# Recurrent attention with a gated layer behind it: transposes of eleven units as DMA transfers in SyncE's queue, and a new order of all stages

## The chip, the core and the metric

The kernel runs on one core of one Trainium2 chip. The metric is device microseconds of one execution (lower is better). Engines: TensorE (PE in the profile; PEld is its weight load), VectorE (DVE), ScalarE (ACT), GpSimd (POOL) and SyncE (SP), which here only issues DMA transfers. One program execution was profiled; its span is the time from the first to the last instruction.

## The reference

Two stages. The first is a linear recurrence for 4 batches, 8 heads, 768 steps and head width 48; the second is a feed-forward layer on the first one's output, 3072 tokens by 384, hidden width 1024.

```
for t in range(S):                     # r, k, v, w: [4, 8, 768, 48], u: [8, 48]
    y[t]  = r[t] @ (state + (u * k[t]) outer v[t])
    state = w[t] * state + k[t] outer v[t]
x  = y as [3072, 384]
h  = x @ w_in                          # [3072, 1024]
s  = h * softmax(h)
ln = (s - mean(s)) / sqrt(var(s) + 1e-6) * g_ln
out = ln @ w_out                       # [3072, 384]
```

## The kernel before

**Tiling.** Time is cut into 6 chunks of 128 steps, and a chunk of one batch is a unit: 24 units, unit i being chunk i // 4 of batch i % 4. All 8 heads of a unit are worked on at once. A unit's stages, by the names that the order uses:

- LW, LK, LR, LV (`load_w`, `load_k`, `load_r`, `load_v`): four transfers of 192 KB in pieces of 48 floats, from SP's queue, into rings of 7 buffers (NIO).
- lw (logarithm, ACT), cum (two products with triangular matrices on PE, the running sums), ex (exponential, ACT), kp (`scaled`, DVE: k and r times the decays, bf16, into a ring of 6 buffers, NKP).
- krk and krr (`transposed`): four PE products each with the identity, which turn the scaled k and r, two heads at a time, into PSUM; kr (`transposed_copy`): a copy of the 128 by 1024 result to SBUF into a ring of 6 buffers, on ACT (".a") or DVE (".d"). These three are the stage that the change touches.
- M (`scores`): eight PE products of turned k with turned r; m (`scores_copy`): to SBUF, on DVE with the causal mask, or on ACT, and then sel (`scores_mask`) on POOL applies the mask.
- p, q, dg, dv: the term with u (POOL, POOL, DVE, POOL); vb (`v_cast`): v to bf16.
- Y (`attend`): turned r times state, plus scores times v, in PSUM; y adds dv (".n") or, with ".i", PE adds it with an identity product. S, et, st: the state of the batch for its next chunk (not needed for the last four units).
- X and xT: y turned by PE and copied; H (24 PE products), e (exponential, ACT), he (DVE), hq (square, on ACT, DVE or POOL): the hidden layer; Oa and Ob (`output`): 36 PE products that give the layer's output, its mean and its sums; sq, qm, lv, o: the scaling; out: the store of 192 KB, SP's queue.

Ahead of the units there are the weights: LI (three transfers of `w_in`) and wi (casts), LO (two of `w_out`), gw (its rows times the gain), mn and mc (their column mean) and ce (the mean taken off, eight pieces). No Oa can start before its rows of `w_out` went through LO, gw, mn, mc and ce, and no H before LI and wi. "hot" is a number of idle PE products.

**What sets the order.** `ORDER` is one list of words, written out; the loop at the end of the kernel (line 512) calls one function per word. Each engine carries out its own instructions in the order of the list (`InOrder`, line 84 and 87: every line of the profile has one of these two numbers, so groups are told apart by tiles). SP's queue holds loads and stores in one order, and a store waits there for its `o`, with all that stands behind it. Each transfer in SP's queue also waits for the completion of the one eight places ahead of it.

Of the kernel before, what the change touches and what calls it, by code (L numbers as in the profile page):

```python
# [9 lines left out]
BF16 = mybir.dt.bfloat16  # L10
# [5 lines left out]
ALU = mybir.AluOpType  # L16
# [2 lines left out]


ORDER = """
LW0 LK0 hot3.s3 LR0 LU0 LG0 lw0 LW1 cum0.b0 LK1 hot1.s3 LV0 LR1 p0 us0.s0 LW2 gs0.s3 hot2.s2 LK2 uc0 gc0 ex0 q0
LI0 LR2 lw1 kp0 LW3 cum1.b1 hot1.s3 vb0.a dg0 LV1 ex1 S0.s1 LK3 krk0.s2 p1 hot3.s3 LR3 kp1 LI1 lw2 krk1.s0 LI2
krr0 cum2.b0 LV2 kr0.d hot1.s3 LO0 M0.b1 krr1 LO1 m0.d hot3.s3 kr1.a LW4 LK4 p2 et0 ex2 M1.b1 LR4 hot4.s3 LW5
dv0 kp2 lw3 LV3 Y0.is3 m1.d vb1.p LK5 krk2.s2 y0.a q1 LR5 krr2 wi0.a cum3.b0 LW6 S1.s0 q2 dg1 X0.s3 LV4 ex3 st0
dv1 LK6 dg2 kr2.a kp3 LR6 Y1.is1 LW7 y1.a krk3.s2 LV5 et1 wi1.a krr3 X1.s1 LK7 wi2.d M2.b1 LR7 xT1.a p3 xT0.d
m2.d LW8 H0.b0 LV6 vb2.p kr3.d LK8 dv2 H1.b1 e0 st1 LR8 gw3.p LW9 gw0.p he0 S2.s1 LK9 e1 Y2.is3 q3 LR9 hot3.s2
et2 gw2.p LV7 y2.a dg3 gw7.a gw1.p X2.s2 LW10 he1 M3.b0 gw4.p LV8 lw4 gw6.p LK10 m3.d hq0.a gw5.p cum4.b1 LR10
mn0.s0 ex4 LW11 hq1.d LV9 xT2.a p4 kp4 mc0 H2.b0 lw5 ce7.d ce0.d ce3.d ce5.d krk4.s3 vb3.a cum5.b1 ce4.d e2
ce6.d krr4 S3.s2 ce1.d ce2.d st2 dv3 ex5 Oa0.s0 kr4.a q4 kp5 Y3.is1 Ob0 p5 et3 he2 lw6 y3.a krk5.s3 cum6.b1 sq0  # L30
q5 X3.s1 st3 ex6 M4.b0 qm0 krr5 xT3.d vb4.p Oa1.s2 m4.d kr5.a S4.s1 p6 lv0 kp6 M5.b0 o0.a Ob1 dg4 lw7 out0 et4
dg5 krk6.s3 m5.a dv4 cum7.b1 LK11 st4 Y4.ns0 LR11 krr6 hq2.d sq1 vb5.a H3.b0 LW12 ex7 qm1 q6 y4.d LV10 kr6.d lv1
sel5 LK12 Oa2.s1 kp7 e3 LR12 S5.s0 dv5 LV11 o1.a he3 krk7.s3 lw8 M6.b1 out1 vb6.p krr7 et5 m6.a Y5.is2 LW13 p7
kr7.d cum8.b0 LK13 dg6 Ob2 ex8 sel6 LR13 st5 X4.s3 LW14 y5.a kp8 M7.b1 sq2 dv6 xT4.a LK14 X5.s0 Y6.ns2 lw9 qm2
S6.s3 xT5.d LR14 q7 m7.a y6.d krk8.s0 LW15 cum9.b0 hq3.d X6.s2 LV12 krr8 ex9 H4.b1 p8 kr8.d lv2 kp9 et6 sel7
Oa3.s0 vb7.a st6 e4 xT6.d p9 M8.b0 dg7 S7.s3 lw10 he4 krk9.s2 q8 et7 Ob3 m8.a vb8.p o2.d cum10.b1 sq3 sel8 st7
krr9 out2 ex10 S8.s1 qm3 kr9.d LK15 H5.b0 hq4.a q9 kp10 LV13 p10 et8 lv3 st8 M9.b1 e5 krk10.s3 m9.d Y7.ns2 vb9.p
krr10 Oa4.s1 dv7 lw11 he5 o3.a cum11.b1 kr10.a out3 S9.s0 y7.d LR15 H6.b0 et9 ex11 dg8 p11 st9 kp11 Ob4 e6 dg9
X7.s3 krk11.s2 vb10.p lw12 he6 Y8.ns0 dv8 xT7.a krr11 cum12.b1 hq5.a S10.s3 q10 kr11.d H7.b0 sq4 ex12 qm4 y8.d
dv9 dg10 et10 lv4 q11 X8.s2 kp12 Oa5.s0 e7 vb11.p o4.a M10.b1 dv10 he7 Ob5 lw13 out4 xT8.a p12 LW16 S11.s1 m10.a  # L40
dg11 krk12.s2 st10 cum13.b0 et11 hq6.d krr12 sq5 ex13 H8.b1 qm5 sel10 st11 lv5 kp13 lw14 Oa6.s3 q12 e8 kr12.d
krk13.s1 p13 cum14.b0 hq7.a he8 krr13 Y9.ns2 p14 Ob6 ex14 y9.d kr13.a q13 o5.d M11.b1 Oa7.s2 dg12 out5 sq6 dv11
m11.a kp14 LK16 Y10.ns0 vb12.p X9.s1 LR16 qm6 M12.b0 xT9.a M13.b1 LV14 m12.d lw15 Ob7 LW17 m13.a vb13.p S12.s1
LK17 y10.d sel11 cum15.b0 LV15 et12 X10.s0 st12 H9.b1 ex15 dg13 dv12 xT10.a kp15 lv6 Y11.ns1 sq7 e9 krk14.s0 qm7
y11.d H10.b0 hq8.d lw16 o6.a q14 he9 X11.s1 lv7 krr14 out6 Oa8.s3 p15 e10 LR17 xT11.d kr14.d cum16.b1 o7.a dv13
S13.s1 he10 ex16 Ob8 out7 q15 LV16 hq9.a kp16 krk15.s0 sel13 LW18 M14.b0 Y12.ns2 sq8 m14.a dg14 LK18 krr15
H11.b1 qm8 p16 y12.d LR18 et13 lv8 kr15.d LV17 lw17 vb14.p st13 LW19 M15.b0 e11 Y13.ns2 krk16.s0 y13.d Oa9.s1
m15.a p17 he11 X12.s2 vb15.a krr16 sel14 cum17.b0 xT12.a dg15 Ob9 ex17 o8.d dv14 X13.s2 H12.b1 out8 sq9 xT13.a
qm9 kp17 vb16.p lv9 kr16.d H13.b0 e12 hq10.d dv15 o9.a he12 Y14.ns3 lw18 krk17.s2 out9 q16 Oa10.s0 e13 LK19
y14.d sel15 krr17 LV18 Ob10 he13 kr17.a LR19 S14.s1 LW20 hq12.a hq11.d M16.b1 LK20 M17.b0 q17 dg16 Y15.ns3 LR20  # L50
m16.a Oa11.s2 y15.d dv16 sq10 m17.d lw19 cum18.b1 p18 et14 X14.s3 Ob11 xT14.a qm10 st14 lv10 sel16 H14.b0 sq11
ex18 o10.d qm11 vb17.p dg17 out10 lv11 q18 kp18 Y16.ns3 LV19 e14 X15.s1 Oa12.s0 LW21 p19 y16.d xT15.a LV20 dg18
cum19.b1 lw20 Ob12 he14 LK21 q19 ex19 LR21 S15.s3 vb18.p sq12 o11.a LW22 kp19 krk18.s1 dv17 cum20.b0 et15 LK22
krr18 qm12 ex20 X16.s2 p20 H15.b1 out11 xT16.d kr18.a LR22 kp20 LW23 Y17.ns2 lv12 hq13.d H16.b0 e15 st15 y17.d
p21 o12.a S16.s1 he15 e16 out12 krk19.s3 q20 Oa13.s2 LV21 hq14.a he16 LK23 krr19 Ob13 LR23 lw21 kr19.d et16 LV22
X17.s0 M18.b1 st16 M19.b0 p22 S17.s3 m18.d m19.a Oa14.s1 sq13 et17 xT17.a qm13 dg19 cum21.b0 Ob14 st17 ex21
hq15.d krk20.s0 hq16.a Y18.ns3 dv18 kp21 krr20 H17.b1 sq14 lv13 sel19 y18.d lw22 kr20.d lw23 vb19.p Oa15.s3
o13.d e17 vb20.p qm14 dg20 out13 dv19 M20.b0 lv14 LV23 he17 Y19.ns0 m20.a X18.s2 Ob15 xT18.d sel20 o14.d
cum22.b1 sq15 Oa16.s2 y19.d ex22 out14 qm15 hq17.d krk21.s1 vb21.a X19.s0 kp22 q21 Ob16 lv15 q22 xT19.d cum23.b0
sq16 o15.d krr21 ex23 krk22.s0 qm16 H18.b1 p23 out15 kr21.a kp23 dv20 krr22 dg21 e18 S18.s3 kr22.d H19.b0 dv21  # L60
lv16 he18 o16.a Y20.ns1 et18 e19 out16 krk23.s0 hq18.d M21.b1 Oa17.s2 y20.d m21.a st18 krr23 he19 Ob17 sel21
kr23.a Oa18.s1 dg22 sq17 q23 Y21.ns3 hq19.d X20.s0 M22.b1 xT20.a qm17 vb22.p M23.b0 y21.d lv17 Ob18 m23.d dv22
m22.a S19.s0 sq18 X21.s3 dg23 sel22 H20.b1 et19 o17.d xT21.d out17 vb23.p qm18 st19 Y22.ns2 dv23 e20 H21.b0
y22.d lv18 he20 Oa19.s3 e21 o18.d X22.s0 Y23.ns2 hq20.d xT22.a out18 Ob19 y23.d Oa20.s1 sq19 qm19 he21 lv19
X23.s0 H22.b1 xT23.d hq21.a H23.b0 e22 Oa21.s2 he22 e23 Ob20 he23 hq22.a Ob21 sq20 o19.a qm20 hq23.d Oa22.s0
lv20 out19 sq21 o20.d Oa23.s3 qm21 out20 lv21 Ob22 Ob23 sq22 qm22 o21.d lv22 sq23 out21 qm23 o22.d lv23 out22
o23.d out23
"""

NIO, NLW, NKP, NWK = 7, 10, 6, 4  # L70
# [24 lines left out]
def kernel(  # L95
# [14 lines left out]
    C = 128  # L110
# [3 lines left out]
    HP = H // 2  # L114
# [6 lines left out]
    pe, act, dve, pool, sp = (InOrder(tc, e) for e in (nc.tensor, nc.scalar, nc.vector, nc.gpsimd, nc.sync))  # L121
# [3 lines left out]
    consts = ctx.enter_context(tc.tile_pool(name="consts", bufs=1))  # L125
# [5 lines left out]
    def bank(shape, dtype, slot, name):  # L131
# [19 lines left out]
                       pattern=[[1, C]], channel_multiplier=-1)  # L151
# [3 lines left out]
                       pattern=[[1, C]], channel_multiplier=-1)  # L155
# [3 lines left out]
                       pattern=[[-1, C]], channel_multiplier=1)  # L159
# [1 line left out]
    pool.tensor_copy(out=ident, in_=ident_f)  # L161

    halves = consts.tile([C, C], BF16)
    pool.memset(halves, 0.0)
    pool.memset(halves[0:2, :], 1.0)
    pool.affine_select(out=halves[0:2, :], in_=halves[0:2, :], compare_op=ALU.is_ge, fill=0.0, base=0,
                       pattern=[[1, C]], channel_multiplier=-64)
    pool.affine_select(out=halves[0:2, :], in_=halves[0:2, :], compare_op=ALU.is_gt, fill=0.0, base=64,
                       pattern=[[-1, C]], channel_multiplier=64)
    off_blocks = consts.tile([C, HP, 2], BF16)  # L170
    pool.memset(off_blocks, 0.0)
    pool.memset(off_blocks[0:2], -30000.0)
    pool.affine_select(out=off_blocks[0:2], in_=off_blocks[0:2], compare_op=ALU.not_equal, fill=0.0, base=0,
                       pattern=[[0, HP], [-1, 2]], channel_multiplier=1)

    one_col = consts.tile([C, 2], BF16)
    dve.memset(one_col, 1.0)
# [6 lines left out]
    kp_t = ring("kp", NKP, [C, 2, H, 64], BF16)  # L184
    for j in range(max(NLW, NKP)):
        if j < NLW:
            dve.memset(lw_t[j][:, :, D:], 0.0)
        if j < NKP:
# [2 lines left out]
    dve.memset(mean_w, -1.0 / DF)  # L191
    w2 = consts.tile([128, KF, DM + 1], BF16)
    dve.memset(w2[:, :, DM:], 1.0 / RDF)
    keep = consts.tile([C, C], BF16)
    pool.memset(keep, 1.0)
    pool.affine_select(out=keep, in_=keep, compare_op=ALU.is_gt, fill=0.0, base=0,
                       pattern=[[1, C]], channel_multiplier=-1)

    vb_t = ring("vb", NLW, [C, H, D], BF16)
    p_t = ring("p", 3, [C, H, D], BF16)  # L200
# [20 lines left out]
    mean_sb = consts.tile([128, DM], BF16)  # L221
    ps = {}


    def rows_of(src, i):
        c, b = units[i]
# [94 lines left out]
        pool.tensor_mul(out=q_t[i % 3], in0=p_t[i % 3], in1=u_bc)  # L321

    def v_cast(i, x):
        copy = {"a": act.copy, "p": pool.tensor_copy}[x]
        copy(out=vb_t[i % NLW], in_=v_t[i % NIO][:, :, :D])

    def bonus_sum(i, x):
# [19 lines left out]
        transposed(i, 1, x)  # L347

    def transposed_copy(i, x):
        copy = {"a": act.copy, "d": dve.tensor_copy}[x]  # L350
        copy(out=kr_s[i % NKP], in_=live[i]["kr_ps"])

# [81 lines left out]
            pe.transpose(x_ps[:, j, :], y_t[i % NWK][:, j * 128:(j + 1) * 128], ident)  # L434

    def x_copy(i, x):
        copy = {"a": act.copy, "d": dve.tensor_copy}[x]
        copy(out=xT_t[i % NWK], in_=live[i]["x_ps"])

# [58 lines left out]
    def store(i, x):  # L498
# [1 line left out]
        sp.dma_start(out=out[b * S + c * C:b * S + (c + 1) * C, :], in_=o_t[i % NWK])  # L500

    stages = dict(
        LW=load_w, LK=load_k, LR=load_r, LV=load_v, LU=load_u, LG=load_g, LI=load_w_in, LO=load_w_out,
        us=spread_u, uc=copy_u, gs=turn_g, gc=copy_g, wi=cast_w_in, gw=gain, mn=column_mean, mc=copy_mean,
        ce=centre, hot=warm_up,
        lw=log_w, cum=cumulate, ex=decays, kp=scaled, p=bonus_rk, q=bonus_u, vb=v_cast, dg=bonus_sum, dv=bonus_v,
# [39 lines left out]
```

## Time and profile before

| | before |
|---|---|
| time, median of 3 runs (range) | 157.55 us (157.5 to 158.48) |
| span of the profiled execution | 156.5 us; no time of its own is given beside it, so 157.55 - 156.5 = 1.05 us is taken to lie around a span |
| PE busy | 138.6 us, 89% of the span |
| DVE, ACT, POOL busy | 129.8, 118.4, 103.1 us (83%, 76%, 66%) |
| SP's DMA queue, share of 16 engines | 75.4% of the span |
| granted TensorE clock, mean | 0.978 |

Busy time is what an engine's instructions took. The chain that ended last goes back from the last instruction to what released it, step by step; a stretch of it on one engine means that nothing else held the work up there. SPq is the time of SP's issuing instructions. A list of packets, bytes and the share of the 16 DMA engines' time goes with each DMA queue. PE's span in the table counts idle products too.

### The profile page before, as it was taken

The page shows a single profiled execution, that of the slowest core. Times are in us where ns is not written, and L with a number is a line of the kernel's source. Part 1 is how long each engine was busy: PE and PEld are TensorE (multiplying, and loading weights), DVE is VectorE, ACT ScalarE, POOL GpSimd, SP SyncE. Part 2 cuts the span into 40 slices and gives each one's busy share as a digit, 9 for nine tenths or more (in the row PEclk, how much of TensorE's full clock was granted, in tenths as well). Part 3 has the DMA queues.
Part 4 walks back from the last instruction along what each step waited for, and adds up shares of the span by engine and source line. Part 5 has one row for each costly group of instructions (what it writes and reads, how often), then busy time and mean ns, then how long its engine had stood idle before and what let it go on. Part 6 is the DMA issues. An engine that isn't in the chain of part 4 may idle for free.

```text
span 156.5 us, 5279 instructions
## 1 busy us (share of the span) xinstructions
PE 138.6 (89%) x2161; PEld 108.1 (69%) x2161; DVE 129.8 (83%) x227; ACT 118.4 (76%) x241; POOL 103.1 (66%) x131
## 2 busy tenths in 40 slices
PE   3879859449599999999999999999999989999980
PEld 1244447218378788887879788887978778798750
DVE  5054777737999999999989989999999999997652
ACT  4171786616589998989998998999979869655941
POOL 7442858995809999895999977399249782860000
PEclk9999999857999999999999999999999999999999
DMA  4999999999999979999559696596999611011024
GB/s 95 195 215 237 265 354 298 211 226 175 208 224 187 225 155 241 178 228 222 124 121 224 168 194 159 136 211 142 222 212 225 170 57 53 4 50 54 0 105 151
DMA packets 104825, 27.08 MB, mean 173 GB/s; under 512 B 100313, under 2 KB 104418, under 8 KB 104802
## 3 DMA queue, kind: packets, MB, share of 16 engines
q1 hardware_dynamic: 104802, 26.75, 75.4%
q8 instruction: 17, 0.28, 0.7%
q14 instruction: 6, 0.05, 0.1%
HBM read 22.03 MB, written 4.72 MB: 171 GB/s over the span
## 4 chain that ended last, share of the span: by engine, by line
PE 65%; SPq 10%; DVE 9%; POOL 5%; DMA 5%; issue 3%; ACT 1%; DVEq 0%; POOLq 0%
PE o_ps L87 23%; PE h_ps L87 17%; SPq L87 10%; PE kr_ps L87 5%; DMA wout_f<-in_moe_w_out_dram 5%; PE s_ps L87 5%; PE y_ps L87 5%; POOL w L87 5%; PE m_ps L87 4%; PE cum_ps L87 3%; DVE w L87 3%; PE x_ps L87 2%; DVE o L87 1%; DVE hq L87 1%; PE mean_ps L87 1%
## 5 line engine op out<-in xcount | busy, mean ns | idle before, releaser
L87 PE MATMUL o_ps<-w,he 128*128 128x385 bf16 x192 | 45.9, 325 | 1.9 <-DVE w L87 1.9
L87 PE MATMUL h_ps<-xT,win_sb 128*128 128x128 bf16 x576 | 36.5, 222 | 0.7 <-DVE xT L87 0.7
L87 PEld LDWEIGHTS <-win_sb 128*128 128x128 bf16 x576 | 34.0, 99 | 1.1 <-ACT xT L87 0.7
L87 DVE TENSOR_TENSOR he<-h_ps,e 128x1024 bf16<-128x1024 f32 x24 | 29.2, 1217 | 3.1 <-ACT e L87 2.7
L87 PE MATMUL o_ps<-inv_col,e 128*128 128x1 bf16 x192 | 31.7, 165 | 0.0
L87 POOL TENSOR_TENSOR p<-kr_in 128x384 bf16<-128x384 f32 x24 | 24.5, 1023 | 10.9 <-DMA kr_in<-in_r_dram 10.9
L87 PE MATMUL o_ps<-one_col,hq 128*128 128x1 bf16 x192 | 31.3, 163 | 0.0
L87 POOL TENSOR_TENSOR dv<-vb,dg 128x384 bf16<-128x384 bf16 x24 | 20.5, 856 | 13.8 <-DVE dg L87 11.9
L87 ACT ACTIVATE e<-h_ps 128x1024 bf16<-128x1024 f32 x24 | 24.5, 1020 | 6.6 <-PE h_ps L87 6.4
L87 DVE TENSOR_TENSOR kp<-cum_ps,kr_in 128x768 bf16<-128x768 f32 x24 | 22.8, 948 | 7.5 <-ACT cum_ps L87 7.3
L87 PEld LDWEIGHTS <-hq 128*128 128x128 bf16 x192 | 18.5, 96 | 12.8
L87 POOL TENSOR_TENSOR q<-p,u_bc 128x384 bf16<-128x384 bf16 x24 | 23.7, 990 | 1.6 <-DMA kr_in<-in_k_dram 1.5
L87 ACT ACTIVATE cum_ps<-cum_ps 128x768 f32<-128x768 f32 x24 | 19.2, 802 | 3.7 <-PE cum_ps L87 3.4
L87 PEld LDWEIGHTS <-kp 128*128 128x128 bf16 x272 | 17.5, 99 | 3.9 <-DVE kp L87 1.2
L87 PEld LDWEIGHTS <-e 128*128 128x128 bf16 x192 | 18.4, 96 | 2.4 <-issue 2.0
L87 POOL TENSOR_SCALAR_AFFINE_SELECT m<-m 128x1024 bf16<-128x1024 bf16 x14 | 15.7, 1119 | 6.4 <-ACT m L87 4.0
L87 PE MATMUL kr_ps<-ident,kp 128*128 128x128 bf16 x192 | 18.7, 225 | 0.9 <-DVE xT L87 0.5
L87 PEld LDWEIGHTS <-he 128*128 128x128 bf16 x192 | 18.4, 96 | 1.0
L87 ACT CAST m<-m_ps 128x1024 bf16<-128x1024 f32 x14 | 14.2, 1011 | 1.0 <-PE m_ps L87 1.0
L87 DVE TENSOR_REDUCE dg<-q 128x8 f32<-128x384 bf16 x24 | 12.9, 540 | 1.4 <-POOL q L87 1.4
L87 ACT COPY kr<-kr_ps 128x1024 bf16<-128x1024 bf16 x10 | 10.1, 1014 | 4.1 <-PE kr_ps L87 4.1
L87 DVE TENSOR_TENSOR m<-m_ps,keep 128x1024 bf16<-128x1024 f32 x10 | 12.1, 1215 | 0.9 <-PE m_ps L87 0.9
(82 smaller groups left out, 276.4 us busy)
## 6 DMA issues: line engine op xcount, KB each, us to landing
w_in<-in_w_dram SPq DMA_DIRECT2D x24, 192.0 KB, 3.6
kr_in<-in_k_dram SPq DMA_DIRECT2D x24, 192.0 KB, 3.7
kr_in<-in_r_dram SPq DMA_DIRECT2D x24, 192.0 KB, 3.7
v_in<-in_v_dram SPq DMA_DIRECT2D x24, 192.0 KB, 3.6
out_dram<-o SPq DMA_DIRECT2D x24, 192.0 KB, 2.0
win_f<-in_moe_w_in_dram SPq DMA_DIRECT2D x3, 512.0 KB, 5.6
wout_f<-in_moe_w_out_dram SPq DMA_DIRECT2D x2, 768.0 KB, 8.5
u_row<-in_u_dram SPq DMA_DIRECT2D x1, 1.5 KB
```

The lines of the kernel that those rows point to most:

```text
L87: made = make(*args, **kwargs)
```

## The change

1. For units 13 to 23 the stages krk and krr (eight PE products) and the copy kr are left out. In their place `kr.t` issues one transposing transfer from SP's queue, SBUF to SBUF, which writes what the copy wrote: the scaled k and r of the unit, 128 by 1024 bf16, as eight turned squares of 128 by 128. The built instruction names blocks of 16 rows by 128 columns.
2. All words stand in a new order. On SP the `w_out` halves are loaded ahead of `w_in` (LO1, LO0, then LI0, LI2, LI1); before, `w_in` came first. The number of idle PE products is 40 (21 before), all of them ahead of the first Oa in both.
3. Engines of some stages change. In numbers of units or pieces, before and after: kr on ACT 10 and 5, on DVE 14 and 8, as transfer 0 and 11; hq on ACT 10 and 8, on DVE 14 and 8, on POOL 0 and 8; ce on DVE 8 and 2, on POOL 0 and 6; gw on ACT 1 and 6, on POOL 7 and 2; m on ACT (with sel on POOL) 14 and 12, on DVE 10 and 12; xT on ACT 14 and 8, on DVE 10 and 16; y on ACT 5 and 2, on DVE 19 and 22; o on ACT 11 and 16, on DVE 13 and 8; vb on ACT 6 and 5, on POOL 18 and 17, on DVE 0 and 2.
4. Three constants are made by words of the order (ih, ik), not ahead of it. A transfer for xT is written too; no word uses it.

```diff
 NIO, NLW, NKP, NWK = 7, 10, 6, 4
...
+    def make_halves(i, x):
+        pool.memset(halves, 0.0)
...
+    def make_keep(i, x):
+        pool.memset(keep, 1.0)
...
     def v_cast(i, x):
-        copy = {"a": act.copy, "p": pool.tensor_copy}[x]
+        copy = {"a": act.copy, "d": dve.tensor_copy, "p": pool.tensor_copy}[x]
...
     def transposed_copy(i, x):
+        if x == "t":
+            sp.dma_start_transpose(out=kr_s[i % NKP], in_=kp_t[i % NKP].rearrange("t j h d -> t (j h d)"))
+            return
         copy = {"a": act.copy, "d": dve.tensor_copy}[x]
         copy(out=kr_s[i % NKP], in_=live[i]["kr_ps"])
```

The new order, in two places: up to the last load of `w_in`, and from the last hidden product ahead of the first transfer to the fourth transfer.

```
LR5 LR0 LK0 LW0 lw0 hot7.s0 cum0.b0 ex0 kp0 hot3.s2 krk0.s0 krr0 LR1 LK3 LW1 lw1 cum1.b1 ex1 LK1 LU0 us0.s1 uc0
ih0 LW2 lw2 LR2 LK2 hot1.s3 cum2.b0 ex2 p0 ik0 LV2 kp1 krk1.s2 krr1 p1 kp2 LV0 LG0 hot5.s1 krk2.s3 gs0.s1 vb0.p q1
LW3 krr2 kr0.d dg1 M0.b1 m0.d gc0 LW5 lw5 kr2.a hot6.s1 M2.b0 m2.d p2 q2 q0 dg0 LO1 LK5 LV1 vb2.p dg2 dv0 dv2
kr1.a hot1.s3 M1.b1 m1.d S0.s0 gw5.a lw3 cum3.b0 gw7.a et0 st0 S2.s1 ex3 LR3 kp3 et2 st2 hot4.s2 cum5.b1 ex5
vb1.p dv1 S1.s3 kp5 LW4 krk3.s2 Y1.is0 y1.a lw4 LO0 krr3 kr3.d gw4.a X1.s1 xT1.d Y0.ns0 M3.b0 m3.d krk5.s2 krr5
cum4.b1 kr5.d hot3.s1 M5.b0 p5 gw3.a p3 ex4 q3 LR4 LK4 kp4 hot1.s2 krk4.s1 y0.d q5 LI0 Y2.ns2 krr4 gw6.a LI2 dg3
X0.s0 kr4.a gw1.a gw0.p gw2.p hot5.s1 mn0.s1 M4.b1 p4 q4 wi0.d LI1 m5.d xT0.d wi2.d wi1.a H0.b0 mc0 ce7.d ce2.d
...
LK18 out5 he8 xT11.a dv13 cum18.b1 Y10.ns3 LR18 ex18 kp18 st10 hq8.p Ob6 sq6 y10.d H11.b0 p16 q16 kr13.t M13.b1
qm6 m13.d Y12.ns2 y12.d hq9.a Oa9.s1 X10.s3 xT10.d e11 he11 hq11.p LW19 lw19 cum19.b1 ex19 LR19 LK19 kp19 Ob9
dg15 lv6 sq9 qm9 dg16 Y13.ns2 y13.d LW17 lw17 Oa8.s3 o6.a lv9 o9.d cum17.b0 LK17 LV15 vb15.p H10.b1 ex17 e10 p18
X13.s0 LR17 kp17 xT13.d kr14.t kr15.t Ob8.s sq8 qm8 p19 kr16.t lv8 o8.a he10 q19 X12.s2 Oa11.s1 S15.s0 M14.b0
```

## Prediction

> **What bounds the kernel now.** I read the busy time by stretches first, then the chain that ended last, then its pieces around 40 us, then the transposes, then the DMA queue.
>
> Busy time of each engine by stretch (columns: length, PE, PEld, DVE, ACT, POOL with instruction counts, granted clock, DMA share, GB/s):
>
> ```profile
> 0.00:20.00 20.00, 14.59 (x99) 7.21 (x100) 9.63 (x32) 9.27 (x16) 10.94 (x29) 1.00 0.90 205
> 20.00:40.00 20.00, 13.37 (x164) 9.78 (x165) 13.84 (x20) 11.95 (x21) 16.02 (x16) 0.83 1.04 249
> 40.00:60.00 20.00, 19.07 (x322) 15.10 (x322) 19.50 (x34) 17.12 (x38) 15.27 (x18) 1.00 0.99 200
> 60.00:80.00 20.00, 20.00 (x345) 16.75 (x344) 19.66 (x32) 19.19 (x39) 17.18 (x21) 1.00 0.82 181
> 80.00:100.00 20.00, 19.98 (x361) 17.03 (x358) 18.71 (x31) 18.63 (x39) 16.64 (x20) 1.00 0.80 178
> 100.00:120.00 20.00, 20.00 (x355) 16.53 (x354) 19.39 (x32) 18.06 (x40) 12.81 (x15) 1.00 0.95 201
> ```
>
> From 40 us on PE is never free, DVE hardly. Before that PE has holes, and the DMA engines are full (share 0.90 and 1.04). The chain:
>
> ```profile
> 17.12 7.74 DMA wout_f<-in_moe_w_out_dram
> ...
> 24.95 2.46 POOL w L87 x2
> ...
> 29.49 4.91 POOL w L87 x4
> ...
> 34.44 1.13 PE mean_ps L87 x3
> ...
> 36.39 4.85 DVE w L87 x7
> ...
> 41.28 0.56 PE o_ps L87 x6
> ```
>
> Up to 41.28 us the end hangs on the load of w_out (landed at 17.12 + 7.74 = 24.9), the gain, the mean and its subtraction; from there nearly every piece is PE, to 151.28 (last piece: 146.15, 5.13 long), and a tail of 156.5 - 151.3 = 5.2 us follows. What the transposes take, by stretch (PE, DVE, ACT):
>
> ```profile
> 100.00:120.00 20.00, 2.31 (x24) 0.68 (x1) 1.77 (x2) 1.00 0.95 201
> 120.00:140.00 20.00, 2.31 (x24) 1.37 (x2) 2.03 (x2) 1.00 0.29 79
> ```
>
> The DMA queue (packets, MB, share of 16 engines), first of 44 to 60 us, then of 44 to 120 us, and the issues:
>
> ```profile
> q1 hardware_dynamic: 15585, 3.12, 95.7%
> ```
>
> ```profile
> q1 hardware_dynamic: 63231, 14.16, 87.1%
> ```
>
> ```profile
> w_in<-in_w_dram SPq DMA_DIRECT2D x24, 192.0 KB, 3.6
> out_dram<-o SPq DMA_DIRECT2D x24, 192.0 KB, 2.0
> ```
>
> The queue that gets the new work is the second busiest resource: between 44 and 120 us it idled only 13%, some 10 us.
>
> **What the change removes from PE.** Four transposes are 0.22 to 0.25 us of the chain where PE runs on (43.12: 0.24), eight per unit 0.46, eleven units 5.1 us. Three identity products in Y go too, at about 0.16 on the path (half their 0.33): 0.5. The copies (1.01 on ACT, 0.68 on DVE) lie beside PE. By counts times means, DVE loses some 9 us over all stages (kr 6 x 0.68, hq 6 x 0.82, ce 6 x 0.71, o 5 x 0.61, less xT 6 x 0.35, y 3 x 0.55, m 2 x 1.2, vb and wi 1.4) and ACT about as much; neither takes PE's place.
>
> **The front.** Now w_in comes last. Before, five weight transfers and 15 unit loads were in at 24.9. The new order puts the same weights and 21 unit loads ahead of the end of LI1. A load takes the DMA engines about 0.97 us: from 44 to 60 us, 3.12 MB in 15.3 us of busy queue is 204 GB/s, and 196,608 bytes at that rate are 0.97. So 24.9 + 6 x 1.0 = 31 us. Then the cast (1.06), and ACT's 17 words up to hq1, 11.6 us by their means (four of about 1.0, two exponentials of cum at 0.80, the rest short): 31 + 1.06 + 11.6 = 43.7 for the first Oa, against 41.3. The subtraction ce, six of eight on POOL at 0.86 (the row of dv), with 1.9 of v and dv between, is done by some 38 us and is covered by H and hq. POOL's two constants move between p's while it waits for loads: nothing. In return PE has done more ahead of the first Oa: 3 cum (0.34), 3 transposed units (0.46), 4 M (0.33), 2 Y (0.37), 1 S (0.47), 1 X (0.2), 5.1 us. Gain 5.1 - 2.4 = 2.7; bounds: -4 if the front slips as far as PE's holes let it, +5 if H comes on time. The 19 more idle products all stand in PE's holes.
>
> If PE stays the bound: 156.5 - 5.1 - 0.5 - 2.7 = 148.2 us of span.
>
> **The DMA queue.** This sets the end, I think. From 31 us, up to the transfer of unit 23, the queue must carry 74 loads (0.97), 15 stores and 9 transfers, then that of unit 23. A store: in the last 17 us 864 packets, nearly all stores' rows, took 18.9% of 16 engines, about 66 ns each, 8 per engine: 0.54 us. So 31 + 71.8 + 8.1 + 10 X = 110.9 + 10 X, X being a transfer's time on the queue. Then landing (a store's 2.0 less 0.54: 1.4), PE's work from M23 on (five H at 1.34, twelve halves of O at 0.84, three Y, three X, two M: 19.2) and the tail (5.2): 136.7 + 10 X. To this I add the time in which the queue is empty because a store blocks SP. Before, that was 10 us between 44 and 120, mostly because loads were ahead; behind a late queue I take 4 (0 to 10). End: 140.7 + 10 X.
>
> X is shown by no row. Low end: 262,144 bytes at a store's rate (196,608 in 0.54) is 0.72. Next: 1024 rows of 256 bytes to read; 15.7 ns for a piece of 192 bytes (15.3 us x 16 / 15585) and 66 for 1536 put 256 bytes at 18, 64 per engine: 1.16. High end: a block of 16 rows writes 32 bytes to each partition, 8192 pieces in all; the trace's DMA records show 9.0 ns for the smallest packets, 512 per engine: 4.6. I take 1.16, nearest in form to the 192-byte loads. Issuing on SP lies within X as long as SP spends less than that on one (its plain issues take 0.36 or more). End: 140.7 + 11.6 = 152.3 of span, 1.05 around it: 153.4. Against the median of 157.55 that is 0.974.
>
> The Trainium skill, "DMA: Bandwidth & Descriptors", Latency and other measured facts, gives DMA transposes 261 GB/s measured; that estimate would make X 1.0, the end 150.7 and the time 151.8. Its page "VectorE: DVE Perf Modes" speaks against the change: under The three transpose paths it has 1309 ns for one 128 by 128 square through the DMA, and its rules send such a square to TensorE if PSUM will do. If eight squares simply added up, X would be 10.5 and the time over 240; no run here shows either yet.
>
> **Waits added.** M13, M18, M19, M20, M21 and M23 stand right behind or soon after their transfer, and a waiting M holds all of PE, with S and Y of other units behind it. A waiting transfer (for its kp, and for Y of the unit six before, which frees the buffer) holds all of SP: the next loads and stores. kp and Y are long done for 13 to 19; kr19 and kr20 stand behind out12 and out13, so M19 has some 3 us for queue and landing, its 3.6 like a load's: 0.6 to 1.5 us, within the 4 above.
>
> **Rivals.**
> 1. *The transposing transfer is slow, and the queue carries the end beyond the old time.* Place: SP's queue between kr13 and kr23. Every us of X costs 10. It equals the span before at X = (156.5 - 140.7) / 10 = 1.6, and is slower by over 1% from X = 1.74. At 2.5 the time is 166.8, at 4.6 it is 187.8. For it: pieces of 32 bytes, and blocks that SP may have to issue singly; against it: 192-byte pieces move well on these queues.
> 2. *POOL becomes the bound.* It gets eight hq of 128 x 1024. Nearest rows: the mask of that shape, 1.12, and q of 384 columns scaled up, 2.64; I take dv scaled up, 2.3. From the first Oa to hq21 POOL then has 83.3 + 8 x 0.3 = 85.7 us of work, PE 89 to the Oa behind it. Before, it idled a sixth or more of each stretch. At 10% idle it is 95 against 89: 148.2 + 6.4 = 154.6, time 155.7; at 15%, 161.
> 3. *The queue keeps up, but five M wait 1.5 us each for their landing*: 148.2 + 7.5 = 155.7, time 156.8: no change.
>
> **How the numbers follow.** The measurement tells about 1% (1.6 us) from no change. Forecast: X up to 1.4, or PE the bound, time 149.3 (148.2 + 1.05) to 155.9: 0.47, faster. X of 1.4 to 1.74, POOL at 10 to 12% idle, and rival 3: 0.15, within 1%. X beyond 1.74, or POOL worse: 0.38, slower. The likeliest case gives 153.4, its own range 149.3 to 156. The range for 8 in 10 has 0.05 left out below 149.3, and above it goes to X of 2.6, 168, with 0.15 beyond.
>
> **What will show it.** Right: a transfer's packets take about 1.2 us of 16 engines; the DMA share is 0.95 or more from 31 to 120 us; the first Oa stands at 43 to 45 us; PE waits for kr<-kp transfers sum to under 5 us; POOL is busy over 18 of 20 us. Wrong: a transfer that lands in 6 us or more, SP issues of over 2 us for it, ACT or POOL waiting for w_in, v_in or kr_in after 90 us, or PE holes in front of M.

## The result: slower, with a late front and new holes on PE

The changed kernel takes 162.9 us (161.22 to 163.32, 4 runs) against 157.65 (157.5 to 158.48) for the kernel before beside it: a ratio of 1.0298 [1.0231, 1.0364] (in brackets the 95% interval). Its profiled span is 161.1 us, before 156.5; the forecast was 152.3, as a time 153.4. Some of the experiments below scatter by up to 5.5 us between their own runs; a profile shows one run.

Busy time of each engine by stretch, changed kernel (columns as before):

```profile
0.00:20.00 20.00, 14.73 (x65) 6.51 (x67) 7.34 (x28) 7.66 (x12) 10.07 (x28) 0.74 0.95 204
20.00:40.00 20.00, 16.57 (x207) 10.08 (x206) 18.24 (x27) 14.07 (x27) 16.33 (x18) 1.00 0.96 239
40.00:60.00 20.00, 19.33 (x324) 15.91 (x325) 18.41 (x29) 18.23 (x36) 17.80 (x21) 1.00 0.95 196
60.00:80.00 20.00, 18.81 (x318) 15.25 (x317) 18.07 (x31) 17.62 (x37) 15.24 (x16) 1.00 0.98 201
80.00:100.00 20.00, 18.80 (x320) 15.09 (x317) 18.09 (x30) 15.08 (x34) 17.43 (x18) 1.00 0.99 204
100.00:120.00 20.00, 18.21 (x295) 14.85 (x289) 15.42 (x27) 14.37 (x32) 15.46 (x15) 0.91 1.05 192
```

PE was full from 60 to 120 us before; now it misses over 1 us in each stretch. The DMA share, 0.82 and 0.80 between 60 and 100 us before, is 0.98 and 0.99.

The span splits exactly into four parts: up to the first output product (Oa), busy PE from there to the end of the last one, idle PE in the same stretch, and the tail. The same view over that one stretch, kernel before and then changed kernel:

```profile
38.70:152.50 113.80, 111.01 (x1905) 91.32 (x1901) 106.51 (x177) 97.96 (x206) 77.46 (x89) 1.00 0.71 156
```

```profile
46.20:156.90 110.70, 104.11 (x1717) 83.63 (x1715) 93.46 (x158) 83.55 (x181) 82.95 (x86) 0.98 0.86 175
```

| us | before | changed | difference | forecast if PE bounds (148.2) |
|---|---|---|---|---|
| first Oa starts | 38.7 | 46.2 | +7.5 | +5.0 |
| busy PE behind it | 111.0 | 104.1 | -6.9 | -10.7 |
| idle PE behind it | 2.8 | 6.6 | +3.8 | -2.6 |
| tail | 4.0 | 4.2 | +0.2 | 0 |
| span | 156.5 | 161.1 | +4.6 | -8.3 |

(The forecast's column is its own terms: 43.7 for the first Oa; 5.1 + 0.5 + 5.1 less work; and, since it counted from 41.3, the 2.6 us in which the first Oa before stood half done.) PE was relieved of work, as forecast, though of less. What it gained went into a later start and into waits. The transfers and the queue:

```profile
q1 hardware_dynamic: 116418, 29.64, 86.8%
```

```profile
kr<-kp SPq DMA_TRANSPOSE x11, 3.8
```

86.8% of 161.1 less 75.4% of 156.5 is 21.8 us of 16 engines, 1.98 per transfer. The packet records give 11 x 1024 packets of 256 bytes, 18 ns in the median and 29 in the mean: 1.87 us for a transfer in the mean, 1.3 to 1.5 us for six of the eleven. A transfer lands 3.8 us after its issue in the median (3.2 to 5.4), and issuing it takes SP 1.24 to 2.74 us. What waited after 40 us (us in all, times, longest):

```profile
POOL vb L85 <- DMA v_in<-in_v_dram: 4.6, 3, 2.1
...
PEld L85 <- DMA kr<-kp: 2.8, 3, 1.9
POOL p L85 <- DMA kr_in<-in_r_dram: 2.8, 3, 1.2
...
PE m_ps L85 <- DMA kr<-kp: 2.3, 3, 1.7
```

The weight load (PEld) and the product (PE) of one M wait for the same landing, so the two kr rows are one wait seen twice: 2.8 us in all, not their sum. (Expectations below, of the first, third and fourth batch, add the two rows; their "some 5", 5.1 and 24.7 should be 2.8, 2.8 and 12.8.) In the kernel before, one row after 40 us names a load: POOL's p waited 5.2 us for r, and PE lacked 2.8 us in all. On the chain that ended last, start and length:

```profile
95.15 3.32 DMA kr<-kp
98.47 0.05 issue
98.52 0.42 PE m_ps L85 x8
...
100.76 5.41 DMA kr<-kp
106.17 0.05 issue
106.21 0.40 PE m_ps L85 x8
```

M of unit 15 and M of unit 17 each stand at the landing of a transfer. These are two of PE's three waits for one, 0.6 and 1.9 us; the third is M of unit 23, 0.3. And the front:

```profile
33.07 5.52 DMA kr_in<-in_k_dram
38.60 0.04 DVEq L85
38.63 0.58 DVE he L85
39.21 0.88 DVE kp L85
40.09 0.05 issue
40.13 0.62 PE kr_ps L85 x8
40.75 1.35 PE h_ps L85 x24
```

The second H, which the first Oa needs, stood behind the turning of unit 6, whose k landed at 38.6. ACT had hardly a gap there either. Busy times from its copy of the column mean to the end of the hq that the first Oa needs (ACT is the fourth engine, 10.27 of 10.59 us):

```profile
34.92:45.51 10.59, 9.77 (x161) 7.78 (x160) 9.45 (x13) 10.27 (x19) 7.64 (x10) 1.00 0.94 184
```

### The profile page after: what moved, and what is told of

It is laid out like the page before. It is cut to its first block, busy times and chain, and to the rows that moved or that the text cites. A ratio compares the mean times of both kernels' runs of the same rounds, so it can differ in the third digit from the quotient of the medians.

```text
span 161.1 us, 5136 instructions
## 1 busy us (share of the span) xinstructions
PE 141.2 (88%) x2089; PEld 105.4 (65%) x2089; DVE 125.2 (78%) x218; ACT 112.4 (70%) x231; POOL 113.6 (71%) x137
## 3 DMA queue, kind: packets, MB, share of 16 engines
q1 hardware_dynamic: 116418, 29.64, 86.8%
## 4 chain that ended last, share of the span: by engine, by line
PE 38%; DVE 17%; DMA 17%; ACT 9%; POOL 9%; issue 4%; SPq 3%; DVEq 0%; POOLq 0%; ACTq 0%
PE o_ps L85 12%; PE h_ps L85 11%; DVE kp L85 6%; DMA kr<-kp 5%; DMA kr_in<-in_k_dram 3%; SPq L85 3%; DMA v_in<-in_v_dram 3%; PE y_ps L85 3%; POOL dv L85 3%; PE cum_ps L85 3%; PE kr_ps L85 2%; DMA kr_in<-in_r_dram 2%; POOL q L85 2%; DVE m L85 2%; DMA w_in<-in_w_dram 2%
## 5 line engine op out<-in xcount | busy, mean ns | idle before, releaser
L85 PEld LDWEIGHTS <-win_sb 128*128 128x128 bf16 x576 | 32.8, 98 | 2.1 <-DVE xT L85 1.0
L85 POOL TENSOR_TENSOR p<-kr_in 128x384 bf16<-128x384 f32 x24 | 24.4, 1024 | 7.2 <-DMA kr_in<-in_k_dram 4.4
L85 POOL TENSOR_TENSOR dv<-vb,dg 128x384 bf16<-128x384 bf16 x24 | 19.8, 828 | 6.5 <-DVE dg L85 4.4
L85 POOL TENSOR_TENSOR q<-p,u_bc 128x384 bf16<-128x384 bf16 x24 | 22.4, 943 | 0.7
L85 POOL TENSOR_TENSOR hq<-he 128x1024 bf16<-128x1024 bf16 x8 | 15.1, 1892 | 6.7 <-DVE qm L85 5.0
L85 DVE TENSOR_TENSOR m<-m_ps,keep 128x1024 bf16<-128x1024 f32 x12 | 14.6, 1219 | 3.0 <-PE m_ps L85 2.6
L85 PEld LDWEIGHTS <-kp 128*128 128x128 bf16 x184 | 12.7, 104 | 5.4 <-DVE kp L85 3.1
L85 PEld LDWEIGHTS <-kr 64*128 64x128 bf16 (+1 forms) x272 | 10.3, 96 | 8.1 <-DMA kr<-kp 2.8
L85 POOL CAST vb<-v_in 128x384 bf16<-128x384 f32 x17 | 9.2, 545 | 8.3 <-DMA v_in<-in_v_dram 8.3
L85 POOL TENSOR_SCALAR_AFFINE_SELECT m<-m 128x1024 bf16<-128x1024 bf16 x12 | 13.9, 1166 | 1.1 <-ACT m L85 1.1
L85 DVE TENSOR_TENSOR y<-y_ps,dv 128x384 bf16<-128x384 f32 x22 | 12.1, 551 | 2.6 <-PE y_ps L85 1.6
```

The costliest lines, as they stand in the source:

```text
L85: made = make(*args, **kwargs)
```

## The experiments

**First batch: transfers or order?** Two runs reverse or remove the transfers in the changed order. The first puts eight PE products and a copy back in place of each transfer, in free banks a few words ahead of M.

```diff
- kr13.t M13.b1
+ krk13.s3 krr13
...
+ kr13.a
...
+ M13.b1
```

> The changed order, with the eleven transposes given back to PE (two groups of four products and a copy per unit, in bank gaps of the order some 10 words ahead of M) and no transfer. Queue theory (each transfer takes about 1.8 us of a DMA queue that is full from 31 us on, and that lateness is the loss): the queue loses 20 us of work, PE gains 5.1 us; the span falls from 161.1 to 151-155, time 152-156. Order theory (the new order is slow by itself: late first Oa, hq on POOL): no better than the changed kernel, 162-168 with the 5 us on PE. Landing theory (only the waits of M for a landing, some 5 us, and the lower clock after them, some 3): 158-161.

172.58 us (170.24 to 174.4), ratio 1.0716 [1.0582, 1.0849], above all three ranges expected. The kernel before took 160.5 us (158.4 to 162.83) beside this batch. PE is idle for 10.0 us behind its first Oa, 5.5 of it waiting for the copies kr (DVE's 3.3, ACT's 2.2), so this run prices my placing of the products too. The second leaves the eleven transfers out; M and Y of units 13 to 23 take what was turned for an earlier unit.

```diff
- kr13.t
...
- kr23.t
```

> The changed kernel without the eleven transfers; the turning of k and r of units 13 to 23 is left out, M and Y of those units read what the buffer held before. Queue theory: 148-152 (PE has 5 us less than in the kernel before and the queue 20 us less than in the changed one). Order theory: 160 or more. Landing theory: 154-156.

162.73 us (161.37 to 163.87), ratio 1.0175 [1.0036, 1.0315]: the span is 161.1, as with the transfers. So neither X nor the queue's sum of work sets the end; had they, 20 us of the queue's work less would have shown. The ratio did fall, from 1.0298 to 1.0175, with intervals that overlap: leaving the transfers out may be worth some 2 us. The order is slow without any turning, though PE has 5.1 us less to do than in the kernel before. From its first Oa on:

```profile
48.40:157.00 108.60, 102.57 (x1718) 82.94 (x1715) 93.76 (x157) 84.12 (x181) 82.40 (x86) 1.00 0.68 151
```

6.0 us of PE are idle here too, and the front was 2.2 us later in this run than in the changed kernel's (46.1 to 48.4 over the seven profiles whose front is the same). Part of that chain:

```profile
77.16 5.08 DMA v_in<-in_v_dram
...
85.94 4.39 DMA kr_in<-in_r_dram
...
107.58 5.76 DMA w_in<-in_w_dram
```

Loads that come late stand where the transfers stood. Between them this chain runs through POOL, DVE and ACT as well, and the longest waits of PE itself name DVE and POOL (he 1.6 us, xT 0.8, vb 0.8). Two more runs:

```diff
-            sp.dma_start_transpose(out=kr_s[i % NKP], in_=kp_t[i % NKP].rearrange("t j h d -> t (j h d)"))
+            sp.dma_start_transpose(out=kr_s[i % NKP][:, :HP, :], in_=kp_t[i % NKP][:, 0].rearrange("t h d -> t (h d)"))
```

> The changed kernel with each of the eleven transfers cut to the half that turns k (128 by 512); the turning of r of those units is left out. Queue theory: a transfer takes half, 0.9 us, ten of them free 9 us: time 152-156. Landing theory: landing hardly changes (most of its 3.8 us is not the transfer's own), 160-163. Order theory: 162-163.

163.69 us (162.38 to 165.11), ratio 1.0252 [1.0135, 1.0369]: half the bytes (k is turned, r is left out), no gain.

```diff
- kr13.t
+ kr13.t kr13.t
...
```

> The changed kernel with each of the eleven transfers issued twice in a row into the same buffer (same result). Queue theory: ten more transfers of 1.8 us ahead of the last M: 162.9 + 18 = 178-183. Landing theory: M waits for the second of the two, 1.5 to 2 us more at five or six M: 170-174. Order theory: 163-165.

200.59 us (198.37 and 202.81). It doubles more than the work: the second transfer into one buffer waits on SP for the first, 25.4 us in all, 11 times. The 37.7 us more hold eleven more transfers and eleven waits of SP for a landing, so this run gives no price of a transfer.

**Second batch: the lead of the loads.** In the list the unit loads stand 113 words ahead of their first use in the kernel before, and 8 in the changed one. Theory D: that is what costs.

```diff
- xT2.a hot4.s3 cum9.b0 ex9 ... H1.b1 e1 LR9 LK9
+ q0 LW9 dg0 LO1 LK5 ... kp3 LR9 LK9 et2
...
```

> The changed kernel, with nothing altered but where the unit loads (units 7 and later) stand in the order: on average 109 words ahead of their first use (8 in the changed kernel, 113 in the kernel before), and at least 12 words after their buffer is free. All eleven transfers are kept. Theory D (the loads' short lead in SP's queue, behind stores that wait for o, is what costs the time, and the transfers themselves little): 153 to 157 us, ratio 0.97 to 1.0, and the waits of ACT, POOL and PE for w_in, v_in, kr_in after 44 us sum to under 5 us. Rival theory Q (the DMA queue is bound by its work, a transfer taking 1.9 us on it): 140.7 + 18.7 + 1.7 of the late front + 1 = 162, as the changed kernel. Rival theory O (the order of the compute stages costs the time): 160 or more as well, told from Q by the run without the transfers.

> As the run before it, loads early, and the eleven transfers left out: the turning of scaled k and r of units 13 to 23 is not done, M and Y of those units take what was turned for an earlier unit. Theory D: 149 to 153, a few us under the run with the transfers. Theory Q: 150 to 154 too, but then the run with transfers stands 8 us or more above this one. Theory O: 160 or more, as without the transfers in the changed kernel's own order.

> As the first, loads early, but the eleven transposes are back on PE (eight products each, copies on ACT and DVE): what the transfers are worth with the loads out of the way. Theory D: 155 to 159, 2 to 5 us above the run with the transfers (5.1 us of PE work comes back, and 7 to 9 us of copies on ACT and DVE). Theory Q: under the run with the transfers. Theory O: 165 or more (172.6 was measured in the changed kernel's own order).

170.87 us, ratio 1.075 [1.0659, 1.0842]; 164.99, 1.0409 [1.0349, 1.0468]; 180.76, 1.1393 [1.1263, 1.1523]. All missed, partly because of the edit itself: the loads went ahead of `w_in`, and the first Oa came at 55.4, 55.8 and 54.6. But in the second of them, without transfers, PE behind the first Oa has 1.6 us of holes (103.3 less 101.7):

```profile
55.80:159.10 103.30, 101.68 (x1718) 82.65 (x1715) 93.39 (x156) 83.75 (x181) 82.64 (x86) 1.00 0.63 142
```

The last run of the batch makes the loads of the kernel before late, and changes nothing else.

```diff
- kp3 LR6 Y1.is1 LW7 y1.a krk3.s2
+ kp3 LR6 Y1.is1 y1.a krk3.s2
...
```

> The kernel before, with nothing altered but the loads of units 7 and later, which are moved down the order to 8 words ahead of their first use on average (113 before). The reverse of the first run. Theory D: 165 or more, ratio 1.05 or above, DMA waits of POOL and ACT for v_in and w_in appear. Theories Q and O: no change from the kernel before, 0.99 to 1.01, since work and compute order are the same.

183.16 us (179.52 to 183.59) with 158.29 beside it. The same work in the same order on every compute engine costs 21 to 25 us more when loads stand 8 words ahead of their use:

```profile
POOL p L86 <- DMA kr_in<-in_r_dram: 27.2, 13, 4.8
...
ACT lw L86 <- DMA w_in<-in_w_dram: 15.0, 7, 4.5
DVE kp L86 <- DMA kr_in<-in_r_dram: 11.5, 7, 4.7
```

**Third batch: the transfers' place.**

```diff
- H11.b0 p16 q16 kr13.t M13.b1
+ lv4 et9 st9 kr13.t vb11.p ... H11.b0 p16 kr16.t q16 M13.b1
...
```

> The changed kernel, with only the eleven transfers moved up the order: ten words behind their kp (29 to 170 words ahead of M, where the changed kernel has 1 to 25). Measured by the ledger of PE from its first output product on, the changed kernel has 104.1 us of busy PE and 6.6 of idle PE, 5.1 of it put down to the landing of a transfer. Theory W (those landings are what costs): idle 1.5 to 3 us, time 157 to 159. Theory L (loads behind stores in SP's queue come late, whatever the transfers do): idle stays at 6, with loads named in place of transfers, time 161 to 163. Theory F (the late front: first output product at 46.2, 38.7 before) holds beside either: nothing below 156 while that product stays at 46.

187.83 us (185.56 to 190.5): wrong by 30. Transfers a few words behind their kp make SP wait for DVE, with all loads behind them:

```profile
SPq L84 <- DVE kp L84: 11.3, 5, 4.8
```

PE waits for no transfer any more. It waits for loads: 6.5 us for lw in front of cum alone, and POOL's p 13.0 us for r. Next, the loads early but behind the last of `w_in`, and then both moves:

```diff
- wi0.d LI1 m5.d ... Y3.is2 y3.a LW9 lw9
+ wi0.d LI1 LW9 LR9 LK9 LW7 m5.d ... Y3.is2 y3.a lw9
...
```

> The changed kernel, with the unit loads of units 7 and later moved up to some 58 words ahead of their use, but none ahead of the last load of w_in (in the first try of early loads they went ahead of the weights and the first output product came at 55.4). Transfers stay where the changed kernel has them. Theory L: idle PE after the first output product 2 to 3.5 us, 157 to 159. Theory W: the transfers still land 1 to 25 words ahead of M, idle 5 or more, 161 to 164.

> Both moves at once. Theories W and L each give what their own move gave; if both kinds of wait have to go, only here idle PE is under 2.5 us and the time 156 to 158. With the first output product at 46 and 102.5 to 104 us of busy PE behind it and a tail of 4.2, theory F forbids less than 155.

175.5 us (171.82 to 176.84), and 167.4 with a ratio of 1.0413 [1.0371, 1.0454]. Both put loads of units 7 and 9 ahead of unit 6's, so the first Oa slid to 53.5 and 54.1. They don't decide on D; the last pair below does. Then the first part of the change alone, in the old order:

```diff
- krk13.s1 p13 cum14.b0 hq7.a he8 krr13 ... kr13.a
+ p13 cum14.b0 hq7.a he8 kr13.t
...
```

> One part of the change alone: the kernel before in its own order, where krr of units 13 to 23 becomes the transfer and krk and the copy go; 9 to 42 words ahead of M. Loads there stand 113 words ahead of their use and the front is the old one. If the new order is at fault (theories L and F) and a transfer costs little: PE's 5.1 us less 0.5 to 2 us of waits, 153 to 156, ratio 0.97 to 0.99. If a transfer costs as much as it saves wherever it stands (landing 3.8 us, SP 1.3 us, the queue 1.9 us each): 157 to 162.

179.38 us, ratio 1.1228 [1.1158, 1.1298]. The first Oa stands at 41.1, and PE behind it is idle for 17.5 us, 12.8 of it in front of M:

```profile
PEld L84 <- DMA kr<-kp: 12.8, 5, 6.9
PE m_ps L84 <- DMA kr<-kp: 11.9, 5, 6.8
```

In an order with good lead for loads, a transfer 9 to 42 words ahead of M stands behind those loads.

**Fourth batch: another queue, the front, fewer transfers.**

```diff
-            sp.dma_start_transpose(out=kr_s[i % NKP],
+            act.dma_start_transpose(out=kr_s[i % NKP],
```

> The kernel before in its own order, transposes of units 13 to 23 as transfers, but issued from ACT's queue, eight words behind their kp (20 to 64 words ahead of M). With the same eleven transfers in SP's queue this order took 179.4 us and PE waited 24.7 us for their landing. If sharing SP's queue is what costs: waits for kr<-kp under 5 us, no loads named, 152 to 158 (ACT gains some 15 us of issuing and loses five copies of 1.0, which lie inside its idle 25%). If the transfer itself costs: waits of 10 us or more, 165 and above.

> The changed kernel with its eleven transfers in ACT's queue at the same words. Without the transfers this order has a span of 161.1 and 6.0 us of idle PE behind the first output product. If sharing SP's queue is the larger cost of a transfer, idle PE is 5 to 6.5 us and the time 159 to 162; if ACT, which then waits for kp and issues for 1.3 to 2.7 us each, becomes the holder, 163 to 168 with ACT named in front of PE.

In the old order 166.22 us, ratio 1.0383 [1.0289, 1.0478]: PE waits for a transfer once, 0.6 us (12.8 us with SP, at 179.4 us), which points to sharing SP's queue as the cost in front of M; the transfers also stand earlier here, 20 to 64 words ahead of M in place of 9 to 42. But the loads now come late (POOL's p waits 16.2 us for r, before 5.2), and the time isn't won. In the changed order 183.16 (178.87 to 183.59): ACT comes to the transfers late, and PE waits 16.7 us for them. Then the loads of unit 6:

```diff
- LW6 lw6 e0 he0 LV3
+ LW6 LR6 LK6 lw6 e0 he0 LV3
...
```

> The changed kernel with one edit: the loads of r and k of unit 6 stand right behind LW6, ahead of LV3 and LW9. In its trace the load of k of unit 6 was issued at 33.07 and landed at 38.6, kp of unit 6 came then, and its transposes (40.13) hold the second hidden product (40.59) behind them in PE's order. If that load holds the front: first output product at 43 to 45 in place of 46.2, time 160 to 161.5. If the DMA engines hold it (their share is 0.97 to there), it stays at 46, time 162.5 to 163.5.

166.59 us (164.67 to 169.61), first Oa at 47.1. Missed: that load was on the chain, but moving it alone frees nothing. ACT is again busy up to the hq of the first Oa, here to 46.45. What holds the front is not settled. And the last units alone, in the old order:

```diff
- hq13.d H16.b0 ... krk20.s0 ... krr20 ... kr20.d
+ hq13.d kr20.t H16.b0
...
```

> The kernel before with only units 20 to 23 turned by transfers in SP's queue, five words behind their kp (31 to 66 words ahead of M), where eight loads or fewer are still to come. PE is relieved of 4 x 0.46 = 1.8 us, ACT and DVE of four copies. If the harm of a transfer in SP's queue is done to the loads behind it, little of it is left here: 155.5 to 158, ratio 0.985 to 1.0, the only one in this study with a chance to beat both. If even here M waits for the landing or the last loads come late: 159 to 164.

162.91 us (158.99 to 163.49) with 158.6 beside it (158.03 to 159.86). It doesn't beat the kernel before even at its best: its shortest run lies within the other's range. In its profile no M waits for a transfer. It shows a stall on DVE instead, 35 us ahead of the first transfer, which SP issues at 119.97 (start, length):

```profile
85.23 4.13 DVE L85 TENSOR_TENSOR hq<-he 128x1024 bf16<-128x1024 bf16 x1
```

The same instruction in the kernel before, whose records of DVE and POOL just ahead of it agree to within some 20 ns:

```profile
85.22 0.79 DVE L87 TENSOR_TENSOR hq<-he 128x1024 bf16<-128x1024 bf16 x1
```

The run of 158.99 has no profile, so whether it had this stall is not known, and this run says little of four transfers.

**Last pair: the lead alone.** The loads behind `w_in` go into the order of their use, 58 words ahead of it; then the transfers also move, to 24 to 47 words ahead of M.

```diff
- LI1 m5.d ... et1 st1 LW6 lw6 e0 he0 LV3
+ LI1 LW6 LV3 LW9 LR6 LK6 LR9 LK9 LW7 m5.d ... et1 st1 LV4 lw6 e0 he0
...
```

> The changed kernel, with the loads behind the last one of w_in put into the order of their first use, 58 words ahead of it on average (8 in the changed kernel), so that fewer of them stand behind stores; the loads of unit 6 keep their place among them. Transfers and all other words unmoved. Theory D (late loads): first output product at 46 to 47, idle PE behind it 3 to 5 us, 158 to 160. If the order of loads against stores does not matter: 162 to 164. If the transfers now land still later because more loads stand ahead of them: waits for kr<-kp of 8 us or more and 165 to 170, and then a transfer's price is what stands ahead of it in the queue.

> As the run before it, and the eleven transfers moved up as well, to 24 to 47 words ahead of M (1 to 25 in the changed kernel) and 15 or more words behind kp, so that SP should hardly wait for kp. Theory D with the waits W together: idle PE 2 to 4 us, 157 to 159. If each of the two moves harms the other, as in the runs of the second and third batch: 164 to 170, with both kr<-kp and v_in or kr_in among the waits.

172.42 us, ratio 1.0856 [1.0799, 1.0912], and 170.49, 1.0715 [1.063, 1.0799]. In the first, the front held (46.7), and no load is among the ten longest waits; POOL's vb still waits 4.6 us for v, as in the changed kernel. In their place:

```profile
PEld L84 <- DMA kr<-kp: 12.4, 4, 6.6
PE m_ps L84 <- DMA kr<-kp: 11.6, 3, 6.4
```

SP's queue ahead of the longest of them (start, length):

```profile
88.00 0.67 SPq L84 DMA_DIRECT2D out_dram<-o  x1
88.71 0.43 SPq L84 DMA_DIRECT2D kr_in<-in_k_dram  x1
89.19 1.50 SPq L84 DMA_DIRECT2D kr_in<-in_r_dram  x1
90.79 1.80 SPq L84 DMA_TRANSPOSE kr<-kp  x1
```

PE ended its last product at 88.1 and stood until 94.57, while SP issued loads and a store ahead of the transfer. This is D's mirror: with early loads the transfer is late, and PE waits over four times the 2.8 us of the changed kernel. In the second, both kinds of wait are there, as its last expectation has it: 8.4 us of PE for transfers, and 2.5, 1.9 and 1.1 us of DVE's kp, POOL's vb and POOL's p for loads.

## Why the prediction was wrong

- **The step that failed** is in "The DMA queue": "This sets the end, I think", and then "To this I add the time in which the queue is empty because a store blocks SP ... behind a late queue I take 4 (0 to 10)", with 0.6 to 1.5 us for a waiting M inside it. It took SP's one queue for a pipe whose end is a sum of work. With no transfer, X = 0, that sum ends at 140.7; the run without transfers has a span of 161.1. What the queue costs is whose turn comes when. With no work changed, moving words in that queue gave 183 in place of 158 (loads late, old order), 188 in place of 163 (transfers early) and 172 in place of 163 (loads early). No allowance of 4 us has that size. Shown: late loads stop POOL, ACT and DVE; a transfer in front of loads stops the loads for its kp; loads in front of a transfer stop M. In the changed kernel itself the loss is smaller: 7.5 us of later front where 5.0 were forecast, and 6.6 us of idle PE where 0.2 were; 2.8 of these stand in front of M for a transfer, and 6.0 are there without any transfer.
- **X** was mis-sized: 1.16 forecast, 1.87 measured. By the prediction's own formula the span would be 140.7 + 18.7 = 159.4, near the measured 161.1, but that is chance: with no transfer at all, where the formula has 140.7, the span is 161.1 too. The median packet of 256 bytes took 18 ns, as interpolated; the mean, 29, made the difference.
- **The pages.** The Trainium skill, "DMA: Bandwidth & Descriptors", Latency and other measured facts, led to an estimate of 1.0 us; the records have 1.87 in the mean and 1.3 to 1.5 for six of the eleven. Its page "VectorE: DVE Perf Modes", The three transpose paths, would make it 10.5 if squares added up; they don't.
- **PE's work.** Removed: yes. Of the 10.7 us forecast 6.9 show behind the first Oa, and 8.4 in the run without transfers, whose clock stayed at 1.00 there. 1.5 to 2 us is the clock (below); the other 2.3 isn't traced.
- **The front**: 46.2, not 43.7. The forecast led the first Oa through `w_in` and ACT. That path is in the trace: ACT's cast of `w_in` ends at 33.5 (32.1 forecast), ACT then waits 1.4 us for PE's column mean, and its words up to hq1 end at 45.5. The chain goes through a load of unit 6 instead, but moving that load up left the first Oa at 47.1. No run makes ACT's work there shorter, so which of the two holds the front stays open. As a gain of 2.7 us it isn't there; the forecast also counted from 41.3, where the first Oa before started at 38.7.
- **Rivals.** Rival 1 has the right side, and X passed its 1.74, but its mechanism fell with the run without transfers. Rival 2: POOL is busy 15 to 18 of 20 us and its hq takes 1.89; over the whole it doesn't bound, but from 133.9 to 142.5 us the chain runs through POOL's work alone, and PE lacks 1.1 us between 133 and 143. Rival 3 is partly there: three waits of M, 2.8 us in all, where it had five of 1.5, but it let everything else keep up. Of the six M that "Waits added" names, only M23 waited, 0.3 us; M15 and M17 had the rest.
- **The signs.** Two of the signs of being right came, a DMA share of 0.95 or more from 40 to 120 us and under 5 us of waits for transfers, and the forecast was wrong all the same. Three signs of being wrong came: issues on SP of over 2 us (to 2.74), waits after 90 us of POOL for v_in (2.9 us) and of ACT for w_in (1.5), and holes in front of M. The waits alone don't tell: POOL waited 5.2 us for r there in the kernel before.
- **Worth of the transfers.** In the changed order, transfers beat my own placing of PE transposes by 7 to 10 us (172.58 and 162.9; against the kernel before beside each, 1.0716 and 1.0298); in the old order they lose 20 (179.38 and 159.24). That fits an order built around them that pays for it elsewhere; no run shows it.
- **Open.** That the 6.0 us of holes in the order without transfers are late loads is indicated by its chain and by the 1.6 us with early loads, but there the front was 7 us later, which also gives loads time. The run that would settle it, loads in the order of use and no transfers, is missing. Nor was the new order run with the old choice of engines, so what the moves to POOL, ACT and DVE cost or gain by themselves is not shown. No order was found in which loads, transfers and front are all on time, and no version beat the kernel before.

## What to carry to other kernels

A transfer between two stages of one unit was a latency of some 4 us here (3.8 in the median), in a queue that works in order: before summing its work, list what stands ahead of it there and what stands behind it, and ask when each is needed. Where that queue also streamed loads and stores at a DMA share near 1, as here, one of the two was late in every order tried. Test a change that comes with a new order by leaving the new operation out: if the time stays, look for the cause in the order.

## What the runs showed of the hardware

After a wait PE ran slower for a while. Behind the landing at 106.17 of the changed kernel PE ran at half clock for some 3.4 us; the third number from the end is the granted clock:

```profile
104.00:108.00 4.00, 2.26 (x33) 1.33 (x31) 1.94 (x3) 2.45 (x3) 4.00 (x5) 0.84 1.05 228
108.00:112.00 4.00, 4.00 (x61) 3.36 (x58) 2.39 (x5) 3.12 (x9) 2.77 (x3) 0.73 1.17 187
```

(0.16 + 0.27) x 4 / 0.5 = 3.4 us, in which PE's work took 1.7 us longer. The wait was 1.9 us long. The Trainium skill, "TensorE: Matmul & The Clock Gate", HAM oscillation, warns of idle gaps over about 3.4 us; here half clock followed a shorter one. That this wait alone set it off isn't shown. Nor does the time show the loss plainly: the four runs of the changed kernel had mean granted clocks of 0.958 (the one profiled), 0.997, 0.96 and 0.992, and spans of 161.1, 160.7, 161.3 and 159.2 us.

A DVE product that takes both inputs from SBUF can stand still for as long as POOL works. In the run with four transfers hq took 4.13 us in place of 0.79: POOL ran without a gap to 88.82, and hq ended 0.5 us later, at 89.36; in the kernel before hq ran at once, and POOL's q took 1.36 in place of 0.92. The two starts of hq differ by 10 ns. POOL in the run with four transfers, to the end of its run of work:

```profile
85.44 0.92 POOL L85 TENSOR_TENSOR q<-p,u_bc 128x384 bf16<-128x384 bf16 x1
86.30 1.10 POOL L85 TENSOR_SCALAR_AFFINE_SELECT m<-m 128x1024 bf16<-128x1024 bf16 x1
87.36 1.01 POOL L85 TENSOR_TENSOR p<-kr_in 128x384 bf16<-128x384 f32 x1
88.30 0.52 POOL L85 CAST vb<-v_in 128x384 bf16<-128x384 f32 x1
```

The same hq in the old order with eleven transfers in SP's queue:

```profile
86.42 4.12 DVE L84 TENSOR_TENSOR hq<-he 128x1024 bf16<-128x1024 bf16 x1
```

With the transfers in ACT's queue it started at 85.91 and took 2.30. POOL's work without a gap ended in these two runs at 89.99 and 87.68, and hq at 90.54 and 88.21, each time some 0.5 us later. The Trainium skill, "GPSIMD Engine Reference", Specifications, says that POOL shares its SBUF interfaces with DVE, with contention when a DVE instruction has two SBUF inputs; it gives no size, and these three runs do.
